# An FFT filter ahead of an MLP: one transform factor as constant 48x48 blocks on four 64x64 tiles

## The chip, the cores and the metric

The kernel runs on one core of a Trainium2 chip. The metric is the device time of one execution in microseconds (us), taken as the median of several runs. A kernel's executions can come in a fast and a slower state. PE is TensorE, PEld its weight loads, DVE is VectorE, ACT is ScalarE, POOL is GpSimd, SP is SyncE, which issues most of the DMAs here.

## The reference

Eight batches of 3008 x 256 go through a real FFT along the 3008, a product with a complex filter (1505 x 256), and the inverse FFT. All 24064 rows then go through an MLP with ELU.

```python
X = np.fft.rfft(x, axis=1)                    # x: (8, 3008, 256)
Y = X * (filt_r + 1j * filt_i)[None]
y = np.fft.irfft(Y, n=3008, axis=1).reshape(24064, 256)
h = y @ w_in                                  # w_in: 256 x 2048, float64 in DRAM
g = np.where(h > 0, h, np.exp(np.minimum(h, 0)) - 1)
out = (g @ w_out).astype(np.float32)          # w_out: 2048 x 256
```

## The kernel before

3008 = 47 x 64, so the FFT is two factors: A over n2 (64 values) and B over n1 (47 values), with a pass through DRAM between them. The twiddles are folded into B, so B has its own 96 x 128 matrix for each of the 32 values of k2. The inverse has the mirror image of B, called the back product here, then the last factor N. Everything is FP32.

```python
def b_unit(b, i):                              # two values of k2
    for u in range(2):
        k = 2 * i + u
        nc.tensor.matmul(ps[:, u, :], wb[:, k, :], t2s[b, k // 4][:, k % 4, :], start=True, stop=True)
    # real part on partitions 0-63, imaginary part on 64-127: four products of 64 partitions
    nc.vector.tensor_tensor(out=s1[lo], in0=ps[lo], in1=f[lo], op=ALU.mult)
    # ... three more on VectorE, then one addition on GpSimd
def bi_unit(b, i):
    for u in range(2):
        nc.tensor.matmul(ps[0:KR, u, :], wi[:, 2 * i + u, :], s[:, u, :], start=True, stop=True)
    # ... one copy on ScalarE
```

The MLP works in slots: `up` (2 matmuls of 512 columns into ph, ELU on DVE and ACT), then `down` of two slots earlier (4 matmuls of 256 columns into po). Each batch has 96 slots. The transform of batch b+1 is spread over the slots of batch b through a plan. Batch 0 has no MLP to hide under, and that makes the start. The weights come as float64 and are converted on DVE by nine instructions for each of 16 pieces. The filter lies in SBUF throughout.

```python
for q in range(4):                             # the four quarters of the weights
    s = (-90, -24, -12, 1)[q]
    for dt in range(2):
        at(s + 2 * dt, w_in_load, q, dt)       # fetch and convert together
        at(s + 2 * dt + 1, w_out_load, 4 * q + 2 * dt)
```

Of the kernel before, what the change touches and what calls it, by code (L numbers as in the profile page):

```python
# [10 lines left out]
FP32 = mybir.dt.float32  # L11
U32 = mybir.dt.uint32
AXT = mybir.ActivationFunctionType
ALU = mybir.AluOpType

# [10 lines left out]
H = 24  # L26
K2 = 32
SL = 48
KR = 2 * SL
HALF = 64  # L30
XC = 4
NXC = H // XC
NB = K2 // 2
NQ = K2 // 4
XBUFS = 4
GBUFS = 4


def _make_tables():







    n2 = np.arange(N2)
    wa = np.zeros((P, P))
    wai = np.zeros((P, P))
    for h in range(2):  # L50
        r = slice(h * 64, h * 64 + 64)
        for k2 in range(K2):
            c = np.cos(2 * np.pi * ((n2 * k2) % N2) / N2)
            s = np.sin(2 * np.pi * ((n2 * k2) % N2) / N2)
            wa[r, h * 64 + k2] = c
            wai[h * 64 + k2, r] = c * (1.0 if k2 == 0 else 2.0)
            if k2 == 0:
                alt = 1.0 - 2.0 * (n2 % 2)
                wa[r, h * 64 + 32] = alt
                wai[h * 64 + 32, r] = alt  # L60
            else:
                wa[r, h * 64 + 32 + k2] = -s
                wai[h * 64 + 32 + k2, r] = -2.0 * s
    n1 = np.arange(N1)
    wb = np.zeros((KR, K2, P))
    wi = np.zeros((P, K2, KR))
    re, im = slice(0, N1), slice(SL, SL + N1)
    for k2 in range(K2):
        for s in range(48):
            if s < 24:  # L70
                k, sign, q = k2 + 64 * s, 1.0, s
            else:
                j = s - 23
                k, sign, q = 64 * j - (k2 if k2 else 32), -1.0, 32 + s - 24
                if j == 24 and k2:
                    continue
            th = 2 * np.pi * ((n1 * k) % N) / N
            c, sn = np.cos(th), np.sin(th)
            if k == 0 or k == NF - 1:
                sn = np.zeros(N1)  # L80
            if k2:
                wb[re, k2, q] = c
                wb[im, k2, q] = sign * sn
                wb[re, k2, HALF + q] = -sn
                wb[im, k2, HALF + q] = sign * c
                wi[:, k2, :] = wb[:, k2, :].T / N
            else:
                src = re if s < 24 else im
                wb[src, 0, q] = c
                wb[src, 0, HALF + q] = -sn  # L90
                m = 1.0 if k in (0, NF - 1) else 2.0
                wi[q, 0, src] = m * c / N
                wi[HALF + q, 0, src] = -m * sn / N
    return [t.astype(np.float32) for t in (wa, wai, wb, wi)]
# [3 lines left out]
def kernel(  # L98
# [11 lines left out]
    wa_d, wai_d, wb_d, wi_d = [  # L110
        nc.inline_tensor(t, name=n).ap() for t, n in zip(_make_tables(), ("wa_t", "wai_t", "wb_t", "wi_t"))
# [9 lines left out]
    sp = pool("sp", 3)  # L121
    t3p = pool("t3p", 2)
    t4p = pool("t4p", 2)
    zp = pool("zp", 2, space=bass.MemoryType.DRAM)
    yd = pool("yd", 2, space=bass.MemoryType.DRAM)
    yp = pool("yp", 3)
    op = pool("op", 3)
    psH = pool("psH", 2, space=bass.MemoryType.PSUM)
    psO = pool("psO", 1, space=bass.MemoryType.PSUM)
    psM = pool("psM", 4, space=bass.MemoryType.PSUM)  # L130

    wa = glob.tile([P, P], FP32, name="wa")
    wai = glob.tile([P, P], FP32, name="wai")
    wb = glob.tile([KR, K2, P], FP32, name="wb")
    wi = glob.tile([P, K2, KR], FP32, name="wi")

    filt = glob.tile([P, K2, D], FP32, name="filt")
# [3 lines left out]

    xs, t1s, t2s, ss, t3s, t4s, zs, yds, ys, g_of, po_of, os_ = ({} for _ in range(12))



    def x_load(b, c):
        t = xs[b, c] = xp.tile([P, XC, D], FP32, tag="xc", name="xc")
        last = c == NXC - 1
        if last:
            nc.gpsimd.memset(t[64:P, XC - 1, :], 0.0)  # L150
        rows = x[b].rearrange("(n2 n1) d -> n2 n1 d", n1=N1)
        for h in range(2):
            w = XC - 1 if (last and h) else XC
            lo = h * H + c * XC
            nc.sync.dma_start(t[h * 64:h * 64 + 64, 0:w, :], rows[:, lo:lo + w, :])

    def a_unit(b, i):
        c, r = divmod(i, XC // 2)
        if r == 0:
            t1s[b, c] = t1p.tile([P, XC, D], FP32, tag="t1", name="t1")  # L160
        ps = psM.tile([P, 2, D], FP32, tag="mx", name="psa")
        nc.tensor.matmul(ps, wa, xs[b, c][:, 2 * r:2 * r + 2, :], start=True, stop=True)  # L162
        nc.scalar.activation(out=t1s[b, c][:, 2 * r:2 * r + 2, :], in_=ps, func=AXT.Copy)  # L163
# [4 lines left out]
    def z_write(b, c):  # L168
        if c == 0:
            zs[b] = zp.tile([KR, K2, D], FP32, tag="z", name="z")  # L170
        t = t1s.pop((b, c))
        for h in range(2):
            for ri in range(2):
                p0 = h * 64 + ri * 32
                r0 = ri * SL + h * H + c * XC
                nc.sync.dma_start(zs[b][r0:r0 + XC, :, :].rearrange("n k d -> k n d"), t[p0:p0 + 32, :, :])

    def z_read(b, j):
        t2s[b, j] = t2p.tile([KR, 4, D], FP32, tag="t2", name="t2")
        nc.sync.dma_start(t2s[b, j], zs[b][:, 4 * j:4 * j + 4, :])  # L180

    def b_unit(b, i):
        ps = psM.tile([P, 2, D], FP32, tag="mx", name="psb")
        for u in range(2):
            k = 2 * i + u
            nc.tensor.matmul(ps[:, u, :], wb[:, k, :], t2s[b, k // 4][:, k % 4, :], start=True, stop=True)  # L186
        f = filt[:, 2 * i:2 * i + 2, :]
        lo, hi = slice(0, HALF), slice(HALF, P)
        s1 = sp.tile([P, 2, D], FP32, tag="s1", name="s1")
        s2 = sp.tile([P, 2, D], FP32, tag="s2", name="s2")  # L190

        nc.vector.tensor_tensor(out=s1[lo], in0=ps[lo], in1=f[lo], op=ALU.mult)  # L192
        nc.vector.scalar_tensor_tensor(out=s2[lo], in0=ps[hi], scalar=-1.0, in1=f[hi],  # L193
                                       op0=ALU.mult, op1=ALU.mult)
        nc.vector.tensor_tensor(out=s1[hi], in0=ps[lo], in1=f[hi], op=ALU.mult)  # L195
        nc.vector.tensor_tensor(out=s2[hi], in0=ps[hi], in1=f[lo], op=ALU.mult)  # L196
        nc.gpsimd.tensor_tensor(out=s1, in0=s1, in1=s2, op=ALU.add)  # L197
        ss[b, i] = s1

    def bi_unit(b, i):  # L200
        s = ss.pop((b, i))
        ps = psM.tile([P, 2, D], FP32, tag="mx", name="psi")
        for u in range(2):
            nc.tensor.matmul(ps[0:KR, u, :], wi[:, 2 * i + u, :], s[:, u, :], start=True, stop=True)  # L204
        if i % 2 == 0:
            t3s[b, i // 2] = t3p.tile([KR, 4, D], FP32, tag="t3", name="t3")
        u0 = i % 2 * 2
        nc.scalar.activation(out=t3s[b, i // 2][:, u0:u0 + 2, :], in_=ps[0:KR], func=AXT.Copy)  # L208

    def y_write(b, j):  # L210
        if j == 0:
            yds[b] = yd.tile([K2, KR, D], FP32, tag="yd", name="yd")
        nc.sync.dma_start(yds[b][4 * j:4 * j + 4, :, :].rearrange("u r d -> r u d"), t3s.pop((b, j)))

    def y_read(b, m):
        t = t4s[b, m] = t4p.tile([P, 4, D], FP32, tag="t4", name="t4")
        for h in range(2):
            for ri in range(2):
                p0 = h * 64 + ri * 32
                r0 = ri * SL + h * H + 4 * m  # L220
                nc.sync.dma_start(t[p0:p0 + 32, :, :], yds[b][:, r0:r0 + 4, :])

    def n_unit(b, m, dh):
# [3 lines left out]
        for q in range(4):  # L227
            nc.tensor.matmul(ps[:, ts(q, P)], t4s[b, m][:, q, ds(dh * P, P)], wai,  # L228
                             start=True, stop=True)
# [4 lines left out]
    def up(b, m, jt):  # L234

        w = 512 if m < 5 else 448
# [28 lines left out]
    def o_store(b, m):  # L265
        rows = out[b * N:(b + 1) * N, :].rearrange("(n2 n1) d -> n2 n1 d", n1=N1)
        for a, o in enumerate(os_.pop((b, m))):
            for h in range(2):
                w = 1 if (a and h and m == 5) else 2
                lo = h * H + 4 * m + 2 * a  # L270
                nc.sync.dma_start(rows[:, lo:lo + w, :], o[h * 64:h * 64 + 64, 0:w, :])
# [3 lines left out]
    def w_load(dst, *srcs):  # L275


        wd = t1p.tile([P, 512, 2], U32, tag="t1", name="wd")
        for i, s in enumerate(srcs):
            n = 512 // len(srcs)  # L280
            nc.scalar.dma_start(wd[:, ts(i, n), :].rearrange("p a w -> p (a w)"), s)
        lo, hi = wd[:, :, 0], wd[:, :, 1]
        m = sp.tile([P, 512], U32, tag="s1", name="wm")
# [38 lines left out]
    with tc.manual_schedule():  # L322
        nc.scalar.dma_start(wa, wa_d)
        for c in range(XBUFS):
            x_load(0, c)
# [87 lines left out]
```

## Time and profile before

| | before |
|---|---|
| median | 3169.59 us (3169.05 to 3171.67, 3 runs) |
| one batch in the steady state | 375.85 us |
| B and back product, matmuls a batch | 32 + 32 of 256 columns, 27.6 us of PE |
| first n1 product of batch 0 | 91.9 us |
| first ELU instruction of the MLP on DVE | 184.1 us |
| PE without gaps from | about 224 us |

The length of a batch is read as the distance between the same instruction of two neighbouring batches: the first back product after 560 us starts at 792.03, the next batches' at 1167.88 and 1543.72. The prediction shows the lines that carry the rest. In a timeline line the columns are start, length, engine, source line, operation, out<-in, tile of the array, elements, count; what stands in brackets is the idle time before it and what ended that.

### The profile page before, as it was taken

The page shows a single profiled execution, that of the slowest core. Times are in us where ns is not written, and L with a number is a line of the kernel's source. Part 1 is how long each engine was busy: PE and PEld are TensorE (multiplying, and loading weights), DVE is VectorE, ACT ScalarE, POOL GpSimd, SP SyncE. Part 2 cuts the span into 40 slices and gives each one's busy share as a digit, 9 for nine tenths or more (in the row PEclk, how much of TensorE's full clock was granted, in tenths as well). Part 3 has the DMA queues.
Part 4 walks back from the last instruction along what each step waited for, and adds up shares of the span by engine and source line. Part 5 has one row for each costly group of instructions (what it writes and reads, how often), then busy time and mean ns, then how long its engine had stood idle before and what let it go on. Part 6 is the DMA issues. An engine that isn't in the chain of part 4 may idle for free.

```text
span 3171.7 us, 28669 instructions
## 1 busy us (share of the span) xinstructions
PE 3034.9 (96%) x11200; PEld 2061.7 (65%) x11200; DVE 1491.4 (47%) x2241; ACT 660.7 (21%) x1137; POOL 170.1 (5%) x148
## 2 busy tenths in 40 slices
PE   2559999999999999999999999999999999999999
PEld 0336677666776666766676667766677666676666
DVE  3663374334733356333653337333473335633443
ACT  0112222221222222222222222222222222221211
POOL 0200020000200011000100002000020001100000
PEclk7779999999999999999999999999999999999999
DMA  9521221112211222021221122111220112210000
GB/s 191 142 78 46 68 57 42 38 47 60 66 28 45 60 60 60 20 59 53 67 54 26 53 62 62 37 39 47 63 68 22 45 40 56 58 26 14 20 7 13
DMA packets 97880, 166.59 MB, mean 53 GB/s; under 512 B 13592, under 2 KB 63512, under 8 KB 97568
## 3 DMA queue, kind: packets, MB, share of 16 engines
q1 hardware_dynamic: 92672, 150.00, 18.1%
q10 hardware_dynamic: 4336, 11.67, 1.4%
q0 software_dynamic: 736, 3.09, 0.6%
q8 instruction: 89, 1.46, 0.2%
q14 instruction: 47, 0.39, 0.0%
HBM read 89.72 MB, written 74.97 MB: 52 GB/s over the span
## 4 chain that ended last, share of the span: by engine, by line
PE 93%; DVE 3%; DMA 3%; issue 0%; SPq 0%; ACT 0%; POOL 0%; ACTq 0%; DVEq 0%; POOLq 0%
PE po L257 42%; PE ph L239 40%; PE psb L186 3%; PE psi L204 3%; PE psn L228 3%; PE psa L162 2%; DMA wd<-in_moe_w_in_dram 2%; DVE s L196 0%; DVE s L193 0%; DVE s L195 0%; DMA wi<-wi_t 0%; DVE s L192 0%; DVE wf L292 0%; DVE we L299 0%; DMA xc<-in_x_dram 0%
## 5 line engine op out<-in xcount | busy, mean ns | idle before, releaser
L257 PE MATMUL po<-w_out,g 128*128 128x256 f32 x6144 | 1453.5, 379 | 0.0
L239 PE MATMUL ph<-y,w_in 128*128 128x512 f32 (+1 forms) x3072 | 1422.2, 585 | 31.7 <-DVE g L245 31.7
L257 PEld LDWEIGHTS po<-w_out,g 128*128 128x128 f32 x6144 | 1163.3, 190 | 386.9 <-issue 259.0
L243 DVE TENSOR_SCALAR g<-ph 128x512 f32<-128x512 f32 (+1 forms) x768 | 522.7, 681 | 1050.6 <-PE ph L239 1049.1
L244 ACT ACTIVATE g<-g 128x512 f32<-128x512 f32 (+1 forms) x768 | 476.8, 621 | 2346.3 <-DVE g L243 2346.3
L239 PEld LDWEIGHTS ph<-y,w_in 128*128 128x128 f32 x3072 | 584.7, 191 | 429.3 <-issue 355.8
L245 DVE SCALAR_TENSOR_TENSOR g<-g,ph 128x512 f32<-128x512 f32 (+1 forms) x768 | 520.1, 677 | 527.4 <-ACT g L244 527.4
L197 POOL TENSOR_TENSOR s<-s,s 128x512 f32<-128x512 f32 x128 | 162.4, 1269 | 1575.9 <-DVE s L196 1514.1
L186 PE MATMUL psb<-t,wb 96*128 96x256 f32 x512 | 134.1, 385 | 22.1 <-DMA t<-z 22.1
L162 PE MATMUL psa<-xc,wa 128*128 128x512 f32 x192 | 104.2, 633 | 51.5 <-ACT t L163 32.4
L204 PE MATMUL psi<-s,wi 128*96 128x256 f32 x512 | 134.4, 385 | 14.8 <-POOL s L197 14.8
L204 PEld LDWEIGHTS psi<-s,wi 128*96 128x96 f32 x512 | 82.9, 165 | 91.8 <-issue 56.6
L228 PEld LDWEIGHTS psn<-wai,t 128*128 128x128 f32 x768 | 102.8, 196 | 54.5 <-issue 41.6
L186 PEld LDWEIGHTS psb<-t,wb 96*128 96x128 f32 x512 | 98.8, 193 | 49.0 <-issue 32.9
L228 PE MATMUL psn<-wai,t 128*128 128x128 f32 x768 | 103.5, 279 | 11.9 <-DMA t<-yd 11.9
L192 DVE TENSOR_TENSOR s<-psb,filt 64x512 f32<-64x512 f32 x128 | 86.6, 677 | 26.7 <-PE psb L186 26.1
L162 PEld LDWEIGHTS psa<-xc,wa 128*128 128x128 f32 x192 | 36.8, 203 | 93.2 <-issue 57.9
L196 DVE TENSOR_TENSOR s<-psb,filt 64x512 f32<-64x512 f32 x128 | 89.0, 695 | 1.8
L193 DVE SCALAR_TENSOR_TENSOR s<-psb,filt 64x512 f32<-64x512 f32 x128 | 88.7, 693 | 1.7
L195 DVE TENSOR_TENSOR s<-psb,filt 64x512 f32<-64x512 f32 x128 | 87.5, 684 | 1.7
L208 ACT ACTIVATE t<-psi 96x512 f32<-96x512 f32 x128 | 74.0, 578 | 63.1 <-PE psi L204 63.1
L163 ACT ACTIVATE t<-psa 128x512 f32<-128x512 f32 x96 | 55.6, 586 | 59.2 <-DMA z<-t 48.4
(26 smaller groups left out, 206.6 us busy)
## 6 DMA issues: line engine op xcount, KB each, us to landing
z<-t SPq DMA_DIRECT2D x192, 128.0 KB, 3.2
t<-z SPq DMA_DIRECT2D x64, 384.0 KB, 3.6
yd<-t SPq DMA_DIRECT2D x64, 384.0 KB, 3.0
t<-yd SPq DMA_DIRECT2D x192, 128.0 KB, 3.0
out_dram<-o SPq DMA_DIRECT2D x184, 128.0 KB, 2.3
xc<-in_x_dram SPq DMA_DIRECT2D x88, 256.0 KB, 4.0
wd<-in_moe_w_in_dram ACTq DMA_DIRECT2D x8, 512.0 KB, 4.6
wd<-in_moe_w_out_dram ACTq DMA_DIRECT2D x16, 256.0 KB, 4.1
```

Source lines behind the costliest of these rows:

```text
L162: nc.tensor.matmul(ps, wa, xs[b, c][:, 2 * r:2 * r + 2, :], start=True, stop=True)
L186: nc.tensor.matmul(ps[:, u, :], wb[:, k, :], t2s[b, k // 4][:, k % 4, :], start=True, stop=True)
L193: nc.vector.scalar_tensor_tensor(out=s2[lo], in0=ps[hi], scalar=-1.0, in1=f[hi], op0=ALU.mult, op1=ALU.mult)
L196: nc.vector.tensor_tensor(out=s2[hi], in0=ps[hi], in1=f[lo], op=ALU.mult)
L197: nc.gpsimd.tensor_tensor(out=s1, in0=s1, in1=s2, op=ALU.add)
L204: nc.tensor.matmul(ps[0:KR, u, :], wi[:, 2 * i + u, :], s[:, u, :], start=True, stop=True)
L228: nc.tensor.matmul(ps[:, ts(q, P)], t4s[b, m][:, q, ds(dh * P, P)], wai, start=True, stop=True)
L239: nc.tensor.matmul(ph[:, 0:w], w_in[:, dt, ts(jt, P)], ys[b, m][:, dt, 0:w], start=(dt == 0), stop=(dt == 1))
L243: nc.vector.tensor_scalar(out=g[:, 0:w], in0=ph[:, 0:w], scalar1=0.0, scalar2=None, op0=ALU.min)
L244: nc.scalar.activation(out=g[:, 0:w], in_=g[:, 0:w], func=AXT.Exp)
L245: nc.vector.scalar_tensor_tensor(out=g[:, 0:w], in0=g[:, 0:w], scalar=1.0, in1=ph[:, 0:w], op0=ALU.subtract, op1=ALU.max)
L257: nc.tensor.matmul(po[q // 2][:, q % 2, :], g[:, ts(q, P)], w_out[:, jt, :], start=(jt == 0 and q % 2 == 0), stop=(jt == JT - 1 and q % 2 ...
```

## The change

The pair n1 and 47-n1 is loaded as one pair of partitions. The tables of A and N carry the twiddles and take sum and difference of the pair. What is left of B are cosines and sines that do not depend on k2. So one small set of 48 x 64 tables serves all k2, and four values of k2 go at once: rows 0 to 47 hold one half, rows 64 to 111 the other, and each feeds two column halves. The products then run on full 128 partitions. These tables are constant, but A and N now have one per pair of n1. The value k2 = 0 keeps a table of its own, so in the group that holds it some matmuls are split in two of 256 columns. The filter is rearranged once in DRAM and read by pieces in every batch. The weights get their own buffers and a new plan.

```diff
-    def b_unit(b, i):
-        ps = psM.tile([P, 2, D], FP32, tag="mx", name="psb")
-        for u in range(2):
-            k = 2 * i + u
-            nc.tensor.matmul(ps[:, u, :], wb[:, k, :], t2s[b, k // 4][:, k % 4, :], start=True, stop=True)
+    def b_unit(b, g):
+        t, f = t2s.pop((b, g)), fbufs[(b * NG + g) % FBUFS]
+        re, im = (psM.tile([P, 2, D], FP32, tag="mx", name=n) for n in ("psr", "psi"))
+        for o, a in ((0, 0), (64, 2)):
+            for ps, k in ((re, LO), (im, HI)):
+                tile_mm(ps[o:o + 64], gb, k, t[:, a:a + 2, :], g == 0 and a == 0)
+        # ... four products of 128 partitions, two additions on GpSimd
...
+        for o, table, sv in ((0, gr, s[0]), (64, gi, s[1])):
+            for ps, k in ((pa, LO), (pb, HI)):
+                tile_mm(ps[o:o + 64], table, k, sv, g == 0 and k == LO)
...
+                at((-96, -48, -24, -22)[q], fetch, *a)
+                at((-95, -47, -23, 2 * j)[q], convert, *a)
...
+            for g in range(NG + 2):
+                s = t + 54 + 2 * g
+                if g >= 2:
+                    at(s, bi_unit, b, g - 2)
+                    at(s, y_write, b, g - 2)
+                if g < NG:
+                    at(s, b_unit, b, g)
```

## The prediction

> **What bounds the kernel now.** I read the page first, top down: the busy table, the slices, the chain of waits, the groups.
>
> ```profile
> PE 3034.9 (96%) x11200; PEld 2061.7 (65%) x11200; DVE 1491.4 (47%) x2241; ACT 660.7 (21%) x1137; POOL 170.1 (5%) x148
> ...
> PE   2559999999999999999999999999999999999999
> PEld 0336677666776666766676667766677666676666
> DVE  3663374334733356333653337333473335633443
> ...
> PEclk7779999999999999999999999999999999999999
> DMA  9521221112211222021221122111220112210000
> ...
> PE 93%; DVE 3%; DMA 3%; issue 0%; SPq 0%; ACT 0%; POOL 0%; ACTq 0%; DVEq 0%; POOLq 0%
> ```
>
> There are two stages. From the fourth slice on, PE is at 9 and nothing else is: TensorE is the bound, and an instruction taken off it there is time taken off the span. The first three slices (79 us each) are a start with PE at 2, 5, 5; there DMA (9, 5, 2) and DVE matter. Since a busy PE need not be PE at its peak, I next took the step between matmul groups from the timeline of PE alone in the middle:
>
> ```profile
> 1163.57 1.03 PE L186 MATMUL psb<-t,wb 96*128 96x256 f32 x4
> 1164.43 1.89 PE L257 MATMUL po<-w_out,g 128*128 128x256 f32 x8
> 1166.16 1.88 PE L239 MATMUL ph<-y,w_in 128*128 128x512 f32 x4
> 1167.88 1.03 PE L204 MATMUL psi<-s,wi 128*96 128x256 f32 x4
> 1168.74 1.03 PE L186 MATMUL psb<-t,wb 96*128 96x256 f32 x4
> 1169.61 1.89 PE L257 MATMUL po<-w_out,g 128*128 128x256 f32 x8
> ```
>
> The starts are what to read. ph x4 takes 1166.16 to 1167.88, 1.72 us: 0.431 us for 512 columns in one record. psi x4 takes 0.86, psb x4 0.87: 0.216 us for 256 columns. Each matmul instruction leaves two records (line 257 issues 4 for each of 768 tiles and has 6144), so a 512-column FP32 matmul costs 0.862 us of PE time, and a 256-column one 0.431, whether the array is used as 128*128, 96*128 or 128*96. No gap stands between kinds: weight loads (0.19 us) are hidden. One batch repeats every 376 us (from the same place in the chain: 764.60 to 1140.44). Third, the stretches of the start:
>
> ```profile
> 0.00:92.00 92.00, 18.45 (x25) 6.44 (x25) 24.72 (x37) 7.80 (x13) 5.54 (x13) 0.69 0.92 192
> 92.00:143.00 51.00, 35.85 (x128) 23.68 (x128) 44.08 (x64) 9.20 (x16) 20.24 (x16) 0.90 0.37 99
> 143.00:184.00 41.00, 9.24 (x40) 6.71 (x40) 35.00 (x72) 2.68 (x5) 0.00 (x0) 0.62 0.50 151
> 184.00:224.00 40.00, 28.42 (x81) 16.87 (x81) 25.80 (x50) 5.24 (x9) 0.00 (x0) 0.78 0.22 66
> ```
>
> Columns: stretch, its length, busy time of PE, PEld, DVE, ACT and POOL, clock, DMA share, GB/s. Up to 92 us DMA is full (0.92, 192 GB/s). Then the frequency product of batch 0 runs at DVE's pace (44 of 51). Then eight weight conversions hold DVE (35 of 41) and the first MLP tile waits for them. Then four more conversions and their loads mix with the first tiles. PE is full from about 224.
>
> **What the Trainium skill says.** "TensorEngine Tiling (Array Packing)", Key Properties: different tiles can load weights and multiply in parallel, and changing the tiling mode drains the engine. No tile of 64x64 is in this trace, so neither is tested yet. "TensorE: Matmul & The Clock Gate", Part 3: matmuls on different tiles run at once, but start and end in program order. That matters here: two records per matmul would, if each waits for the one before it on its tile, hold back the next tile. "FP8 and Floating Point Precision", TensorE Precision Notes: true FP32 is four passes; the trace agrees in that the two records of a 512-column matmul, 0.862 us together, are four times 512 columns at the 2.4 GHz that the clock-gate page gives (0.853). "DMA: Bandwidth & Descriptors", on the semaphore increment of 16: a transfer runs on the largest number up to 16 of DMA engines that divides its slowest dimension. The new filter copies have 23 there, so one engine each; the old ones split 23 into 16 and 7. No trace shows the new ones yet.
>
> **The change part by part, steady state (batches 1 to 7, under the MLP of the batch before).** The A factor: 12 matmuls of 512 columns become 24 of 256 with own weights. Columns are the same, 24 x 0.431 = 10.3 us a batch, and its extra weight loads (0.19) hide behind 0.216. N keeps its 48 matmuls. The MLP is the same; the narrow tile of 448 moves from block 5 to block 0. So only the n1 factor counts.
> Before: 32 + 32 matmuls of 256 columns a batch, 64 x 0.431 = 27.6 us.
> After, by the program's order: 8 groups of four matmuls of 512 columns forward and as many back. If the four tiles really run at once, a group of four costs 0.862 us: 16 x 0.862 = 13.8 us. Gain 13.8 us a batch, 96 us for seven.
> Off this goes the switching. The program puts the back product of group g-2 and the forward product of group g one after the other, so there are 10 visits to the small tiles a batch. One visit has two mode changes. My estimate for one change: a record's modelled length of 378 ns (256 columns) less its step of 216 leaves about 0.16 us to drain; a weight load of 0.19 may show as well. So 0.3 to 0.7 us a visit; I take 0.45. Then 10 x 0.45 = 4.5 us a batch, 31 us for seven. Net steady gain: 96 - 31 = **65 us**.
> DVE: four 128-partition products of some 0.69 us a group of four k2, where there were eight of 64 partitions. 16 x 4 become 8 x 4, 22 us a batch less, but DVE is not the bound. POOL: 16 additions of 1.27 us a batch as before, and 16 filter loads. DMA: 8 x 3.1 MB more, on a share of 0.2: hidden. The loads are asked for four slots (at least 14 us) ahead, landing in some 4 us by the similar loads of z.
>
> **The start.** Bytes wanted before the first n1 product are slightly more: about 17.2 MB before (192 GB/s x 92 us is 17.7), some 19 after, because the filter goes through DRAM once and a second quarter of the weights comes early. Estimate +8 us, first product at about 100. Product stage: DVE needs 8 x 2.76 = 22 us instead of 44, but both product buffers pass through the same four PSUM buffers, so PE and DVE take turns; I estimate 4.3 us a group plus a tail of 5, some 40 us instead of 51: -11. Conversions between product and MLP: four of 4.55 us (the row of conversions in the timeline) instead of eight: -18. The last four are loaded ahead, so their waits of 3 to 4 us (wd in the chain, 186 to 217) vanish: of the 40 us from 184 to 224 PE used 28, and some 7 of the rest come back. Sum: 8 - 11 - 18 - 7 = **-28 us**.
> Total of this path: 3169.6 - 65 - 28 = 3077.
>
> **Rivals.** (1) A staircase: program order holds, the second record of a tile waits for the first, and the next tile starts only with it. Four matmuls then cost five record times, eight in a row nine: 9 x 0.431 = 3.88 us a visit against 8 x 0.431 = 3.45 before. With switching the steady state loses some 0.4 + 0.45 a visit, 8 a batch, 55 us in seven; the start still gives 20 to 25. Result about 3200. For it: the skill's program order and the two records a matmul. Against it: the order of the four matmuls alternates rows, then columns, which is what one does for overlap, and the whole rewrite makes sense only if they overlap. (2) Two at a time: 16 matmuls of four become equal to before; only switching (+31) and the start (-28) remain: about 3170. (3) The filter becomes the wait: its single-engine copies at 12 GB/s (192 over 16) take 15 us each, in three rounds of eight outstanding; the first product would slip to 110 or 120 us, and half of the start's gain is gone: +10 to +20 on any path. Against it: copies fall on different engines and start by about 20 us. (4) The DMA traffic is hidden anyway, and so is POOL: no time.
>
> **Range and chances.** I give the parallel path 0.62 (3040 to 3105 by the price of switching and the filter), rival 1 0.2, rival 2 and mixtures 0.18. Faster by over 2% means under 3106: 0.6. Slower by over 2% means over 3233: only rival 1 with a lost start, 0.06. The middle is 0.34. The point is drawn a little from 3077 towards the rivals: 3082, range 3035 to 3180.
>
> **What would show it.** In the timeline of PE in the middle: a visit of eight matmuls (16 records) in about 2.2 us from the start of its first to the start of the next po right, 3.9 or more wrong. The batch period read from repeated places should fall from 376 to about 366.5. PE full from about 195 us rather than 224. The gap between the last small-tile record and the next 128*128 one gives the switch. The prediction goes wrong most by the tiles not overlapping, then by switches of over 0.5 us each, then by a filter that lands after 105 us.

## The result, and the profile after

The changed kernel takes 3060.76 us (3057.59 to 3063.0, 4 runs), the kernel before 3170.51 us in the same job. The ratio is 0.9653, with a 95% interval of 0.9637 to 0.967. Ratios are taken over the fast runs; they are not quite the ratios of the medians. The outputs are correct. The gain is 109.8 us.

The page of the changed kernel, its busy table, slices and the chain of waits:

```profile
PE 2959.3 (97%) x11456; PEld 1953.6 (64%) x11456; DVE 1300.6 (43%) x1991; ACT 659.8 (22%) x1137; POOL 248.4 (8%) x289
...
PE   2599999999999999999999999999999999999999
...
PEclk7599999999999999999999999999999999999999
DMA  9722230223212231122311223012330213200000
...
PE 94%; DVE 1%; issue 0%; DMA 0%; ACT 0%; POOL 0%; DVEq 0%; SPq 0%; POOLq 0%
```

PE reaches 9 one slice earlier, in the third. It is still the only full engine after that, so the kernel has the same bound with less work for it. DVE lost 191 us of work and POOL gained 78. In the chain DVE falls from 3% to 1% and DMA from 3% to 0%, and POOL stays at 0%.

The timeline of PE alone in the middle, one visit to the small tiles (pva and pvb are the back product, psr and psi the forward one):

```profile
1114.06 1.88 PE L251 MATMUL ph<-y,w_in 128*128 128x512 f32 x4
1115.87 0.64 PE L196 MATMUL pva<-sr,gr 48*64 48x512 f32 x1
1115.88 0.64 PE L196 MATMUL pvb<-sr,gr 48*64 48x512 f32 x1
1115.88 0.64 PE L196 MATMUL pva<-si,gi 48*64 48x512 f32 x1
1115.89 0.64 PE L196 MATMUL pvb<-si,gi 48*64 48x512 f32 x1
1116.35 0.59 PE L196 MATMUL pva<-sr,gr 48*64 48x512 f32 x1
...
1117.21 0.59 PE L196 MATMUL psr<-t,gb 48*64 48x512 f32 x1
...
1117.75 1.99 PE L269 MATMUL po<-w_out,g 128*128 128x256 f32 x8
1119.58 1.88 PE L251 MATMUL ph<-y,w_in 128*128 128x512 f32 x4
```

Four matmuls of different tiles start within 0.02 us of each other. The second records of all four follow together 0.48 us later. The two products, 16 records, last from 1115.87 to 1117.64 (the last group starts at 1117.21 and takes 0.43). The price of the mode change can be read off in four places. ph should end at 1114.06 + 1.72 = 1115.78, and the small tiles start 0.09 later. Their first step is 0.48 instead of 0.43. po starts 0.11 after 1117.64. And po takes 1.83 to the next ph where it otherwise takes 1.725. The sum is 0.35 us a visit. The first forward product of a batch starts at 725.11, of the next at 1090.67: a batch takes 365.57 us, 10.28 less than before. Over seven batches this is **72.0 us**. The other **37.8 us** of the 109.8 come from the start.

The stretches of the start, in the columns that the prediction explains:

```profile
0.00:92.00 92.00, 22.62 (x65) 14.54 (x68) 41.95 (x80) 7.69 (x13) 25.37 (x33) 0.67 0.93 232
92.00:143.00 51.00, 35.04 (x123) 10.07 (x119) 26.45 (x47) 8.68 (x16) 24.92 (x26) 0.50 0.70 191
143.00:184.00 41.00, 32.45 (x130) 23.41 (x131) 32.08 (x64) 8.05 (x15) 0.00 (x0) 0.86 0.33 91
184.00:224.00 40.00, 38.56 (x147) 26.94 (x147) 19.08 (x33) 7.90 (x14) 0.00 (x0) 1.00 0.21 58
```

In the same 41 us from 143 to 184 in which PE had 9 us of work before, it has 32. In the next 40 it has 38.6 instead of 28.4. The first stretch moved 232 GB/s where the kernel before moved 192 at the same DMA share. The second shows the granted clock at 0.50, where the kernel before had 0.90: in the product stage of batch 0 PE now runs at half its clock.

### The profile page after: what moved, and what is told of

It reads as the page before. It is cut to its first block, busy times and chain, and to the rows that moved or that the text cites. A ratio compares the mean times of both kernels' runs of the same rounds, so it can differ in the third digit from the quotient of the medians.

```text
span 3060.0 us, 29380 instructions
## 1 busy us (share of the span) xinstructions
PE 2959.3 (97%) x11456; PEld 1953.6 (64%) x11456; DVE 1300.6 (43%) x1991; ACT 659.8 (22%) x1137; POOL 248.4 (8%) x289
## 2 busy tenths in 40 slices
DMA packets 129610, 192.01 MB, mean 63 GB/s; under 512 B 23452, under 2 KB 97582, under 8 KB 129344
## 4 chain that ended last, share of the span: by engine, by line
PE 94%; DVE 1%; issue 0%; DMA 0%; ACT 0%; POOL 0%; DVEq 0%; SPq 0%; POOLq 0%
PE po L269 43%; PE ph L251 42%; PE psn L241 3%; PE psa L168 2%; PE pva L196 2%; PE psr L196 2%; DVE we L320 0%; ACT g L256 0%; DVE g L255 0%; PE pvb L196 0%; DMA wd<-in_moe_w_in_dram 0%; DMA wd<-in_moe_w_out_dram 0%; DVE g L257 0%; DVE wf L313 0%; DVE we L318 0%
## 5 line engine op out<-in xcount | busy, mean ns | idle before, releaser
L210 POOL TENSOR_TENSOR sr<-sr,sp 128x512 f32<-128x512 f32 x64 | 80.9, 1264 | 1313.3 <-DVE sp L208 1313.3
L241 PEld LDWEIGHTS psn<-tn,t 128*128 128x128 f32 x768 | 102.9, 196 | 59.7 <-issue 59.7
L196 PE MATMUL psr<-t,gb 48*64 48x512 f32 (+1 forms) x272 | 82.2, 626 | 48.5 <-DMA t<-z 48.5
L168 PE MATMUL psa<-xc,ta 128*128 128x256 f32 x384 | 105.5, 402 | 20.9 <-DMA xc<-in_x_dram 18.5
L241 PE MATMUL psn<-tn,t 128*128 128x128 f32 x768 | 103.7, 280 | 15.5 <-DMA t<-yd 15.5
L196 PE MATMUL pva<-sr,gr 48*64 48x512 f32 (+1 forms) x144 | 75.5, 616 | 5.8 <-DVE si L207 4.6
L211 POOL TENSOR_TENSOR si<-si,sq 128x512 f32<-128x512 f32 x64 | 80.8, 1263 | 0.0
L196 PE MATMUL pva<-si,gi 48*64 48x512 f32 (+1 forms) x144 | 75.5, 617 | 0.0
L196 PE MATMUL pvb<-si,gi 48*64 48x512 f32 x128 | 75.5, 673 | 0.0
L196 PE MATMUL pvb<-sr,gr 48*64 48x512 f32 x128 | 75.1, 671 | 0.0
```

What stands on the lines that cost most here:

```text
L168: nc.tensor.matmul(ps[:, u, :], ta[:, 2 * j + u, :], xs[b, c][:, 2 * r + u, :], start=True, stop=True)
L196: nc.tensor.matmul(ps[:, u:u + w, :], table[k, v, :], rhs[k, u:u + w, :], start=True, stop=True)
L210: nc.gpsimd.tensor_tensor(out=sr, in0=sr, in1=p, op=ALU.subtract)
L211: nc.gpsimd.tensor_tensor(out=si, in0=si, in1=q, op=ALU.add)
L241: nc.tensor.matmul(ps[:, ts(q, P)], t4s[b, m][:, i - 4 * m, ds(dh * P, P)], tn[:, i, :], start=True, stop=True)
```

## The experiments

Times to compare with are 3060.8 us and a batch of 365.57 us.

**Whole array instead of tiles.** Is the steady gain TensorE time saved by the tiles? The group's four matmuls become two on all 128 rows and columns. The results are wrong.

```diff
-        for o, a in ((0, 0), (64, 2)):
-            for ps, k in ((re, LO), (im, HI)):
-                tile_mm(ps[o:o + 64], gb, k, t[:, a:a + 2, :], g == 0 and a == 0)
+        for ps, a in ((re, 0), (im, 2)):
+            nc.tensor.matmul(ps, ta[:, g, :], t[:, a:a + 2, :], start=True, stop=True)
 ...                                    # the same for pa and pb; z is read into all 128 rows
```

> Wrong on purpose: the four small-tile matmuls of a group become two matmuls of 512 columns on the whole array (same loads within a few rows, same products, additions, copies). Theory (the steady gain is TensorE columns saved by four tiles at once, less 0.35 us a visit): a batch goes from 365.6 back to about 375.9 us (16 x 0.862 more, 10 x 0.35 less), 72 us in seven batches, total about 3133. Rival (the gain comes from DVE's halved products or from the start, and the tiles matter little): total stays within 10 us of 3061.

Measured: 3127.15 us, and a batch of 375.69 us. PE's timeline shows a visit of the same two products without mode changes:

```profile
1123.17 1.02 PE L218 MATMUL pva<-sr,ta 128*128 128x512 f32 x2
1124.03 1.02 PE L218 MATMUL pvb<-si,ta 128*128 128x512 f32 x2
...
1126.60 1.89 PE L267 MATMUL po<-w_out,g 128*128 128x256 f32 x8
```

The lines left out are the forward product. From 1123.17 to 1126.60 are 3.43 us, against 1.77 on four tiles, or 2.07 there with the mode changes (1115.78 to 1119.58 less 1.725 for po). With DVE's products, the additions and the filter traffic all as in the changed kernel, a batch is back to the length of the kernel before (375.85). So the steady gain is TensorE time, 10.12 of the 10.28 us a batch, and the tiles are what gives it. Of the difference in total, 66.4 us, the batches make 7 x 10.12 = 70.8; the start is some 4 us shorter here. The profiles show where: from the first product to the last copy of the back product this run takes 42.1 us (90.0 to 132.1) at a granted clock of 0.91, the changed kernel 47.5 at 0.50. In the start the tiles save nothing.

**Two tiles only.** Do tiles of one row group run at once, or only tiles of different rows? All matmuls read the lower rows; wrong on purpose.

```diff
-            for ps, k in ((re, LO), (im, HI)):
+            for ps, k in ((re, LO), (im, LO)):
 ...                                    # and pa, pb likewise
```

> Wrong on purpose: all four matmuls of a group read the lower rows, so they fall on two tiles of one row group instead of four. Theory (each tile has its own queue and two tiles of one row group still run at once): a group costs 1.72 instead of 0.86 us, a batch 13.8 us more, 379.4; total about 3061 + 97 and up to 25 more in the cold start, 3160 to 3185. Rival (tiles of one row group share their rows and exclude each other): a group costs 3.45 us, a batch 41 us more, total about 3350 or more.

Measured: 3195.81 us, and a batch of 382.48 us. A back product of this run:

```profile
1181.17 0.64 PE L196 MATMUL pva<-sr,gr 48*64 48x512 f32 x1
1181.19 0.64 PE L196 MATMUL pva<-si,gi 48*64 48x512 f32 x1
1181.65 0.59 PE L196 MATMUL pva<-sr,gr 48*64 48x512 f32 x1
...
1182.08 0.59 PE L196 MATMUL pvb<-sr,gr 48*64 48x512 f32 x1
```

Both tiles read the same 48 rows, and they start 0.02 us apart. The rival, mutual exclusion (3350 us), is out. There is more to see. The program order here is pva of sr, pvb of sr (both on the first tile), then pva of si (on the second). The third of these starts 0.9 us before the second. So records on a free tile start ahead of earlier ones that wait for a busy tile; whether the hardware or the lowering of a matmul into records brings this about, the trace does not show. The batch is longer than expected by 3.1 us. Half of that is the clock: once in this batch a po group of eight (from 1206.36) lasts 3.35 instead of 1.83 us, and just there the granted clock is 0.51 (the column before the last two), where it is 0.99 and 1.00 in the 3.4 us on either side:

```profile
1206.10:1209.50 3.40, 3.40 (x10) 2.53 (x9) 2.48 (x4) 0.00 (x0) 1.04 (x1) 0.51 0.45 116
```

The changed kernel's clock stays at 1.00 throughout its batches. Most of the rest lies in the two visits with the split products of k2 = 0, which take 2.78 and 4.07 us to the next po, 0.9 and 0.5 more than the expectation gives (1.03 + 0.86 and 1.89 + 1.72).

**Another order of the four.** Does the overlap depend on neighbours in the program lying on different rows?

```diff
-        for o, a in ((0, 0), (64, 2)):
-            for ps, k in ((re, LO), (im, HI)):
+        for ps, k in ((re, LO), (im, HI)):
+            for o, a in ((0, 0), (64, 2)):
```

> The four matmuls of a group in another program order: the two tiles of one row group first, then the two of the other. Theory (tiles are independent, records of a later tile pass the second record of an earlier one): total within 5 us of 3061, batch 365.6. Rival (overlap needs neighbours in the program on different row groups): up to 16 x 0.43 us a batch more, 48 us in seven, total up to 3110.

Measured: 3058.02 us, ratio 0.9645 (0.9631 to 0.966), a batch of 365.57 us. The order makes no difference to a batch, and none in total that can be told from the spread of the runs. Only the start looks different: from the first product to the last copy this run's profile has 43.4 us (89.3 to 132.7) instead of 47.5, at the same granted clock of 0.50.

**More visits.** Is the 0.35 us a price of the visit or of the matmul?

```diff
-                    at(s, bi_unit, b, g - 2)
-                    at(s, y_write, b, g - 2)
+                    at(s + 1, bi_unit, b, g - 2)
+                    at(s + 1, y_write, b, g - 2)
```

> The back product goes one slot after the forward product instead of beside it, so the array changes mode for 16 visits a batch instead of 10. Theory (a visit costs 0.35 us of lost TensorE time, whatever is done in it): 6 x 0.35 = 2.1 us a batch, 367.7 instead of 365.6, 15 us in seven, total about 3076. Rival (the loss goes by matmuls, not by visits): total within 4 us of 3061.

Measured: 3078.25 us, a batch of 368.56 us, 2.99 more. Six more visits at 0.35 are 2.1. The waits of PE within that batch show one more thing, and nothing else:

```profile
PE po L269 <- ACT o L273: 0.8, 1, 0.8
```

The columns are us in total, times, longest. Once a batch po waits 0.8 us for the copy of the last output tile, since the visits now fall beside the end of an MLP tile. 2.1 + 0.8 = 2.9 of the 2.99. So the price goes by visits and not by matmuls, of which there are as many as before, and putting forward and back product side by side, as the change does, is worth six of them.

**Filter kept in SBUF.** Are the loads of the filter hidden in the steady state?

```diff
-FBUFS = 3
+FBUFS = 8
...
-                at(t + 49 if g < 2 else s - 4, f_read, b, g)
+                if b == 0:
+                    at(t + 49 if g < 2 else s - 4, f_read, b, g)
```

> The filter is read once and stays in SBUF (eight buffers, loads in batch 0 only), 22 MB less traffic and 112 fewer loads on the POOL queue. Theory (loads asked for 14 us ahead are hidden, TensorE is the bound): total within 4 us of 3061. Rival (the filter traffic or POOL's issuing costs time somewhere): 5 us or more less than 3061.

Measured: 3058.17 us, ratio 0.9646 (0.9633 to 0.966), a batch of 365.57 us. The page's total falls from 192.01 to 169.97 MB, and the batch does not change by a hundredth of a microsecond. The 2.6 us less in total are within the spread (3055.31 to 3062.68). The traffic is hidden in the steady state.

**Old plan of the weights in the changed kernel.** What in the start is due to the new plan?

```diff
-                at((-96, -48, -24, -22)[q], fetch, *a)
-                at((-95, -47, -23, 2 * j)[q], convert, *a)
+                at((-90, -24, -12, 1)[q] + j, fetch, *a)
+                at((-90, -24, -12, 1)[q] + j, convert, *a)
```

> The changed kernel with the weights fetched and converted in the slots of the kernel before (fetch and conversion together, four early, eight between product and MLP, four under the first tiles). Theory (most of the 38 us gained at the start come from the earlier fetch and conversion of the weights): 20 to 35 us slower than 3061, about 3088, and the batch stays 365.6. Rival (the start's gain comes from the shorter product stage and the loads of x): under 8 us slower.

Measured: 3079.47 us, 18.7 more, a batch of 365.57 us. This is a little less than expected. The longest pieces of the chain of waits in the start show what the old plan costs:

```profile
138.63 4.88 DMA wd<-in_moe_w_in_dram
164.35 3.45 DMA wd<-in_moe_w_in_dram
173.06 3.59 DMA wd<-in_moe_w_in_dram
182.35 2.89 DMA wd<-in_moe_w_out_dram
```

The waits for weights under the first MLP tiles (164 to 185 us) are back. But the first n1 product starts at 76.1 us, 12.5 earlier than in the changed kernel, and this is what the new plan costs. Up to the first product the DMA engines move 18.3 MB here (241 GB/s) and 20.7 in the changed kernel (234 GB/s), whose second quarter is fetched ahead of it. My estimate from these: the 2.4 MB are some 10 of the 12.5 us. So bytes ahead of the first product do cost time; how the rest comes about is not shown.

**New plan of the weights in the kernel before.**

```diff
-        wd = t1p.tile([P, 512, 2], U32, tag="t1", name="wd")
+        wd = wds[key] = wp.tile([P, 512, 2], U32, tag="wd", name="wd")
...
+                at((-96, -48, -24, -22)[q], fetch, *a)
+                at((-95, -47, -23, 2 * j)[q], convert, *a)
```

> The kernel before with only the new plan of the weights (own buffers, fetched ahead). Theory: the start gains 18 us from four conversions fewer on the path and 7 to 15 from hidden waits: about 3142, batch unchanged at 375.8. Rival (the early second quarter makes the crowded first 92 us longer and takes the gain back): 3160 or more.

Measured: 3147.57 us, 23.2 under the kernel before in the same job (3170.73), ratio 0.9927 (0.9915 to 0.994), a batch of 375.85 us. This is 5.6 us over the theory's 3142 and clear of the rival's 3160. The first n1 product is later here too (99.0 instead of 91.9 us), the first ELU instruction earlier (174.6 instead of 184.1). From both sides, then, the plan is worth 19 to 23 of the start's 37.8 us.

**Idle banks for batch 0.** In the start forward and back products take turns through four PSUM banks. The two banks of ph are free there.

```diff
+        if b == 0:
+            re, im = (psH.tile([P, 2, D], FP32, tag="ph", name=n) for n in ("psr", "psi"))
+        else:
             re, im = (psM.tile([P, 2, D], FP32, tag="mx", name=n) for n in ("psr", "psi"))
```

> The changed kernel, with the forward products of batch 0 in the two PSUM banks that the MLP does not use yet. Theory (in the start forward and back products take turns through four banks, 4.65 us a group where DVE has 2.5 us of work): 1 to 1.5 us a group less, 8 to 12 us, total about 3051. Rival (the loads of the next stage end the start anyway, or TensorE at its cold clock is the bound there): total within 4 us of 3061.

Measured: 3055.35 us (3053.21 to 3055.67, 5 runs) against 3060.76 (3057.59 to 3063.0), which was measured in another job. The ranges do not overlap, and the first ELU instruction is at 150.6 instead of 157.4 us. But the step from group to group is 4.65 us, as in the middle of the stage without the change. What is better are the last two groups: 4.65 us each where the changed kernel takes 5.22 and 6.40. So the gain is half of what was expected, and the theory was wrong about where it lies. PE's timeline of this run has small-tile records some 0.86 us apart, at a granted clock of 0.54 over this stage; the four steps of a group are 3.4 of the 4.65 us, so in the middle more banks had little to give. Why the end of the stage counts can be seen in ACT's queue. The fetch of the third quarter of the weights stands there behind a copy of the back product. The first line is the changed kernel, the second, in a fence of its own, this run:

```profile
131.36 0.82 ACTq L297 DMA_DIRECT2D wd<-in_moe_w_in_dram  x2
```

```profile
125.20 0.82 ACTq L300 DMA_DIRECT2D wd<-in_moe_w_in_dram  x2
```

The four conversions before the MLP wait for it: they start at 135.67 and at 129.59 us. The run with another order of the four matmuls has 43.4 us from the first product to the last copy without the extra banks, this one 42.8, so the banks are not the only way to the shorter stage.

**Later table.** As the last, with the table of N asked for ten slots later.

```diff
-        at(-48, nc.scalar.dma_start, tn, tn_d)
+        at(-38, nc.scalar.dma_start, tn, tn_d)
```

> The run with the idle banks, and the 1.5 MB table of the last factor fetched ten slots later, when the crowded loads are over. Theory (up to the first n1 product the DMA engines are the bound, at some 230 GB/s): the first product comes 4 to 7 us earlier than 87.6, total about 3050. Rival (the order of the z writes and x loads sets the first product, not the bytes): total within 2 us of 3055.

Measured: 3054.47 us (3053.65 to 3055.43, 5 runs), first product at 87.2 us. This run did not test what it was made for. The first line is the issue on ACT's queue in the changed kernel, the second, in a fence of its own, that of this run:

```profile
51.49 0.47 ACTq L419 DMA_DIRECT2D tn<-tn_t  x1
```

```profile
56.26 0.45 ACTq L422 DMA_DIRECT2D tn<-tn_t  x1
```

The queue of ACT holds nothing to wait for in those ten slots, so the DMA goes out at once behind the weights, 4.8 us later and still 31 us ahead of the product. A slot of the plan is a place in a queue, not a time. The run is the fastest correct version here, level with the run before.

**Weights in the product stage.** As the last, and the second quarter of the weights is fetched at slot -43 and converted at -35, -33, -31 and -29.

```diff
-                at((-96, -48, -24, -22)[q], fetch, *a)
-                at((-95, -47, -23, 2 * j)[q], convert, *a)
+                at((-96, -43, -24, -22)[q], fetch, *a)
+                at((-95, -35 + 2 * j, -23, 2 * j)[q], convert, *a)
```

> As the last, and the second quarter of the weights too is fetched only when batch 0 reads z, and converted between the products of batch 0, where VectorE has 2 of 4.65 us idle. Theory (bytes ahead of the first product cost time, conversions in VectorE's gaps cost little): first product at 75 to 79 us, product stage up to 8 us longer, total about 3046, at least 8 us under 3055. Rival (the conversions delay the products one for one, 4 x 4.55 = 18 us): total 3055 to 3065.

Measured: 3071.57 us, 17.1 more than the last run. The fetch went out at 50.3 us, as early as in that run, so the first product stayed at 87.8 us and the bytes were again not tested. The conversions were. DVE's timeline, a group's last product, the last instruction of the conversion, and the next group's first product:

```profile
115.28 0.68 DVE L212 TENSOR_TENSOR sq<-psi,f 128x512 f32<-128x512 f32 x1
...
121.71 0.69 DVE L325 TENSOR_TENSOR w_in<-wf,we 128x512 f32<-128x512 f32 x1
122.32 0.68 DVE L209 TENSOR_TENSOR sr<-psr,f 128x512 f32<-128x512 f32 x1
```

The groups that have a conversion in front are 8.8 us apart (113.49 to 122.32). The nine instructions are a block in front of the next product and are not spread over DVE's idle time. The rival's mechanism is right, though the total lies above its range: 4 x 4.55 = 18.2 us expected of it, 17.1 measured.

**No filter, both kernels.** What does bringing the filter cost in the start? Zeros take its place; both are wrong on purpose, and single runs of unknown state.

```diff
-        f_load()                # kernel before
-        f_arrange()             # changed kernel, and its f_read with it
```

> Wrong on purpose: the kernel before without the filter loads (zeros instead). Theory (its 3.1 MB into 24 and fewer partitions of SBUF cost more DMA time than other loads, 0.6% of 16 engines' 3172 us, 304 us, 19 us on all 16): first n1 product at about 73 to 76 us instead of 91.9. Rival (the filter costs like any 3.1 MB, 12 us): first product at about 80.

> Wrong on purpose: the changed kernel without the rearranged filter and its loads (zeros instead). Theory (copied within DRAM the filter costs like any 3.1 MB, 12 us on all 16 engines): first n1 product at about 77 us instead of 88.6; batch still 365.6. Rival (the copy costs twice its bytes, or nothing): first product below 70 or above 85.

Measured: 3140.59 us and first product at 60.9 us without it in the kernel before, 31.0 earlier; 3032.82 us and first product at 59.5 us in the changed kernel, 29.1 earlier. The batches keep 375.85 and 365.57 us. Both expectations of the cost (19 and 12 us) were too small. The filter delays the first product by some 30 us either way, more than twice what 3.1 MB take at 232 GB/s (13 us). Two parts can be told apart by an estimate. Up to the first product the changed kernel moves 20.7 MB at 234 GB/s and without the filter 16.2 at 273; the kernel before moves 17.7 at 192 and without it 14.5 at 238. At the rates with the filter, the bytes that fall away are 19 of the 29 us and 17 of the 31; the rest is the lower rate. Part of the mechanism is in the waits of SP's queue of the changed kernel between 40 and 92 us:

```profile
SPq L160 <- DMA wd<-in_moe_w_in_dram: 9.5, 1, 9.5
```

Line 160 loads x and has no use for the weights. The instruction records of the trace show the link: the fetch of weights that ACT issued at 45.82 us counts up semaphore 102, and this load, issued at 55.69, waits for semaphore 102 and nothing else. In these records SP's and ACT's transfers take turns on the same eight semaphores, so one slow transfer on either queue holds back a later one on the other. The z writes stand behind it in the same queue. Up to 95 us SP's queue waits 19.9 us for weights in the changed kernel, and 8.9 us without the filter. How much of the 30 us comes by such waits stays open.

## Why the prediction was right or wrong

The forecast was 3082 us (3035 to 3180), most likely faster by over 2%; measured were 3060.8. The reason given for it, columns of TensorE saved by four tiles at once, holds. Of the terms, the price of a visit was off in size, and in the start two of four were wrong.

- **TensorE is the bound in the steady state: right.** A batch changed by what TensorE had to do; removing filter traffic did not move it, giving TensorE its columns back did (375.69).
- **Four tiles run at once: right.** Starts 0.02 us apart, 0.43 us a step, order of no effect on a batch. The staircase did not happen: the second record of a tile (1116.35) does not hold back the first ones of the others (1115.88). "TensorEngine Tiling (Array Packing)", Key Properties, has it right for FP32 on 64x64 tiles. The program order which I drew from the clock-gate page, and which made the rival, does not hold for the kernel's matmuls in the two-tile run; whether the lowering had changed it is not shown.
- **Ten visits at 0.45 us: right in kind, a little high.** 0.35, by two ways (the timeline of one visit, and 13.79 - 10.28 = 3.51 us a batch over ten). Steady gain 72.0 instead of 65.
- **The start: -37.8 instead of -28,** and its terms were less good than the sum. That the sum came so near is in part luck, since the first row is 11 us better than predicted and the second 7 worse:

| term of the sum | predicted | measured |
|---|---|---|
| first product | +8 | -3.3 (91.9 to 88.6) |
| first product to the last copy of the back product | -11 | -3.9 (51.4 to 47.5) |
| last copy to first ELU instruction | -18 | -19.6 (40.8 to 21.2) |
| from there, waits under the first tiles | -7 | -11.0 (the rest of 37.8) |

The last copies end at 143.3 and 136.1 us, the first ELU instructions start at 184.1 and 157.4. These marks are of one profile each. Five profiles with the same program up to the first product (the changed kernel, two tiles, other order, more visits, idle banks) put it between 85.5 and 89.3 us, so the first row is good to some 4 us. The step that failed in it is the fixed 192 GB/s: I divided the bytes by the rate of the kernel before, and that rate was not a property of the chip (234 after, up to the first product, at about the same share). The bytes were too low as well, 19 MB where 20.7 were moved; at 192 GB/s these would have put the first product at 108 us. The second row failed about as much at the end as before it. A group takes 4.65 us in the middle, where 4.3 were estimated, the last two steps are 5.22 and 6.40, and the tail after the last product is 7 instead of 5. The prediction did not speak of the clock either, which fell from 0.90 to 0.50 in this stage; as the other order takes 43.4 us at 0.50, the clock alone does not make the 47.5. The conversions, the term that rests on counted instructions, came out within 2 us.

- **Rival 3, the filter as the wait: wrong as put.** Its copies had landed and the loads of its first pieces were issued at 73.3 us, 15 us ahead of the first product, which waits for z. Of the 18 copies only eight have 23 rows, not all as the prediction has it. These, of at most 184 KB, took 18.2 us to land in the median where it has 15, and the four of 24 rows with 384 KB took 11.9; that goes the way of the rule that it cites, but the number of engines was not measured. Yet bringing the filter costs the start 29 us by delaying other transfers, and as much in the kernel before, so it does not enter the difference much.
- **Rival 4, traffic and POOL hidden: right** in the steady state.

What stays open is what sets the first product at 88.6 us, beyond the shares of the filter and of the second quarter of the weights: the two runs made to test bytes did not move the transfers, and why the rate differs from kernel to kernel (192 to 273 GB/s) was not tested.

## What to carry to other kernels

If TensorE is the bound and its matrices can be made small constant blocks, try four 64x64 tiles: here they did in 1.77 us what the whole array needed 3.43 for, in FP32. Each visit cost 0.35 us, so put all small-tile work of a stage side by side. Where TensorE was not the bound, in the start, the tiles gained nothing. Cost terms that rest on counted instructions and their own durations held within 2 us here; the one that rested on a transfer rate read from another kernel did not. And before a test of a transfer's timing is believed, look in the trace whether the transfer moved at all.

## What the Trainium skill lacked or had wrong

- "TensorEngine Tiling (Array Packing)", Key Properties, says that a change of mode drains the engine and gives no figure. Here a change there and back costs 0.35 us (0.09 + 0.05 + 0.11 + 0.10), about as much for one product as for two, and six more of them a batch cost 2.2 us (2.99 less a wait of 0.8).
- "TensorE: Matmul & The Clock Gate", Part 3, says that matmuls start in program order. In the order of the kernel's matmuls this did not hold (the lowering may have changed it, which the trace does not show). With FP32, whose matmul leaves two records, a matmul on a free tile started 0.02 us after the first record of a busy tile while an earlier matmul of that tile started 0.91 us after it (1181.19 and 1182.08 against 1181.17). The page does not say how FP32's passes and tiles go together.
- "DMA: Bandwidth & Descriptors" speaks of two transfers on one semaphore as a danger to the data. It does not say that a program which waits for the earlier one lets a transfer on one queue hold up another queue: an x load on SP waited 9.5 us for weights on ACT's queue that it does not use.
- The same page does not give what a load into few partitions or a copy within DRAM costs other transfers: 3.1 MB of filter delayed the start by 31.0 and 29.1 us.
